# An order table of 1036 steps for the attention, gating and first expert units of a fused attention and two-layer-expert kernel

## The chip, the cores and the metric

The kernel runs on one core of one Trainium2 chip. Its time is the device time of one execution in microseconds (us). The core has five engines with instruction queues of their own: TensorE (PE, with its weight loads shown apart as PEld), VectorE (DVE), ScalarE (ACT), GpSimd (POOL) and SyncE (SP, which here only issues transfers). Each queue is worked off in the order in which the program wrote it; the engines wait for each other through semaphores.

## The reference

Three stages follow each other. The first is a linear attention with random features over 4 batches, 8 heads, 576 tokens and head size 64; its result is laid out as 2304 tokens of 512 numbers. The second is a mixture of eight experts in which each token takes the one expert with the largest logit. The third is a plain two-layer network with a squared ReLU.

```python
def phi(x):
    proj = np.einsum('bhsd,md->bhsm', x, omega)
    h = proj - np.sum(x * x, axis=-1, keepdims=True) / 2.0
    return np.exp(h - np.max(h, axis=-1, keepdims=True)) / np.sqrt(m)
kv, z = np.einsum('bhsm,bhsd->bhmd', k_p, v), np.sum(k_p, axis=2)
num, den = np.einsum('bhsm,bhmd->bhsd', q_p, kv), np.einsum('bhsm,bhm->bhs', q_p, z)
x = num / (den + 1e-06)
...
expert_idx = np.argmax(x @ w_gate, axis=1)
out[mask] = gate_w[mask, None] * (np.maximum(xe @ w1[e], 0.0) @ w2[e])
...
h = np.maximum(x @ w_in, 0.0)
return h * h @ w_out
```

## The kernel before

The 2304 tokens are cut into 18 tiles of 128; a batch is four and a half tiles, so tiles 4 and 13 belong to two batches. Every tile passes through the attention twice, as keys (`kp`) and as queries (`qp`).

Of a key tile: TensorE projects it into two banks of the accumulator memory (`proj`, L250), VectorE takes the maximum of each head (`most`, L265, twice), and adds it to half the squared length of the row (`shift` L271, `shifted` L278; the squares come from GpSimd, L197 and L199, and are summed by VectorE at L211, or, for the first five tiles, come from TensorE at L229). ScalarE takes the exponentials of eight heads (`expo`, L291, 8 instructions), and TensorE adds the tile's share to its batch's key-value sums (`kv_part`, L306). When a batch is complete, `kv_close` copies the sums out (L320, L321) and `kvg_turn` and `kvg` (L329, L331, L338, L345) work the gate's weights into them.

A query tile is projected in the same way; then TensorE transposes the exponentials, in two halves (`t_step`, L354), they are copied out (L356), multiplied with the key-value sums (`n_step`, L372), divided on VectorE (`n_den`, `n_rec`, `n_out`, `n_lg`: L386, L390, L396, L401), transposed again (`x_step`, L412) and copied by ScalarE into `xT` (L416), where the experts read them.

The gating makes of the logits the expert of each token, counts per batch the tokens of each expert on TensorE (L502 takes the count), and loads the weights of the batch's busiest expert. An expert unit is a first product (`layer1`, L874 to L876), a split of its result in a high part on ScalarE (L886) and a low part on VectorE (L887), and a second product (`layer2`, L902 to L904). There are 64 such units, numbered from 0; after the second product of each, `extras` issues the loads and splits planned for that unit.

The order of all this is written out in loops in `attention`: five key tiles ahead, then 13 rounds, each with one query tile s, the key tile s + 5 and the later steps of query tiles s - 1 and s - 2, then rounds of query tiles alone, into which the first units and the gating are written by hand. Eight banks are used under fixed names: `k0`, `k1` for key projections, `q0`, `q1` for query projections, `w0`, `w1` for the key-value sums, `t0`, `t1` for transposes and products. So `x_step` and the first half of `n_step` take the same bank:

```python
ps = self.bank("t0", f"x_ps{t}")      # x_step
ps = self.bank(f"t{i}", f"n_ps{t}_{i}")   # n_step
```

An instruction that writes a bank waits until those that read what was there before are done. The transfers of keys, queries and values are issued on SP's queue in the order of the loops; a load waits for its buffer (four for key columns, three for query columns, two for rows, six for values).

Of the kernel before, what the change touches and what calls it, by code (L numbers as in the profile page):

```python
# [15 lines left out]
P = 128  # L16
# [13 lines left out]
SCALE = float(D) ** -0.25  # L30
HW = 96
# [13 lines left out]
F64_MOST = 122880.0 - 2.0 ** -7  # L45

# [45 lines left out]
class Kern:  # L92
# [92 lines left out]
    def load_rows(self, tag, t):  # L185
        if t >= NT:
            return
        pool = self.kpool if tag == "kp" else self.qpool
        x = pool.tile([P, DM], F32, tag=tag + "r", name=f"{tag}r{t}", bufs=2)
        self.nc.sync.dma_start(out=x, in_=self.a["kk" if tag == "kp" else "qq"][t, :, 1, :])  # L190
        self.rows[tag, t] = x

    def squares(self, tag, t):
        if t >= NT:
            return
        x = self.rows[tag, t]
        self.nc.gpsimd.tensor_tensor(x, x, x, ALU.mult)  # L197
        v = x.rearrange("p (h d) -> p h d", h=H)
# [7 lines left out]
    def sums(self, tag, t):  # L206
        if t >= NT:
            return
        sq = self.rows.pop((tag, t)).rearrange("p (h d) -> p h d", h=H)[:, :, 0:32]
        ssq = self.qpool.tile([P, H, 1], F32, tag="ssq", name=f"ssq_{tag}{t}", bufs=3)  # L210
        self.nc.vector.tensor_reduce(ssq, sq, axis=AX.X, op=ALU.add)  # L211
        three = self.trio(tag, t)
        self.nc.gpsimd.tensor_scalar(three[:, :, 1:2], ssq, -0.5 * SCALE * SCALE, None, op0=ALU.mult)
        self.load_rows(tag, t + 2)
        self.squares(tag, t + 1)

    def colsquares(self, t):
        x = self.cols["kp", t]
# [12 lines left out]
    def colsum(self, tag, t):  # L231
        if t > 4:
            return
        at = 4 * VW + SUMS_AT[t]
        ps = self.kv_ps[0, t % 2][:, at : at + H]
        three = self.trio("kp", t)
        self.nc.vector.tensor_copy(three[:, :, 1:2], ps.rearrange("p (h o) -> p h o", o=1))

    def proj(self, tag, t, banks):

        nc = self.nc
        if t >= NT:
            return
        x = self.cols.pop((tag, t))
# [34 lines left out]

    def expo(self, tag, t, r):  # L280

        nc = self.nc
        if t >= NT:
            return
        ps, bias = self.pj[tag, t], self.bias[tag, t]
        if r == 0:
            pool, to = (self.kpool, self.kp) if tag == "kp" else (self.qpool, self.qp)
            to[t] = pool.tile([P, H, M], F32, tag=tag, name=f"{tag}{t}", bufs=3 if tag == "kp" else 2)
        y = (self.kp if tag == "kp" else self.qp)[t]
        for h in range(r, H, 2):  # L290
            nc.scalar.activation(y[:, h, :], ps[r][:, h // 2 * M : (h // 2 + 1) * M], AF.Exp, bias=bias[:, h : h + 1])  # L291
# [4 lines left out]
    def kv_part(self, b, t, i):  # L296
# [18 lines left out]
    def kv_close(self, b):  # L315
        kv = self.kv[b] = self.qpool.tile([P, 2, 4, XW], F32, tag="kv", name=f"kv{b}", bufs=2)
        self.kvn = self.qpool.tile([P, 2, 4, D], F32, tag="kvn", name=f"kvn{b}", bufs=1)
        for i in range(2):
            ps = self.kv_ps[b, i][:, : 4 * VW].rearrange("p (h w) -> p h w", w=VW)
            self.nc.vector.tensor_copy(kv[:, i, :, 0:VW], ps)  # L320
            (self.nc.vector.tensor_copy if b == 0 else self.nc.scalar.copy)(self.kvn[:, i], ps[:, :, 0:D])  # L321

    def kvg_turn(self, b):

        nc = self.nc
        kvn = self.kvn.rearrange("p a h d -> p (a h d)")
# [76 lines left out]
    def x_step(self, t):
        nc = self.nc
        if not 0 <= t < NT:
            return
        ps = self.bank("t0", f"x_ps{t}")
        for i in range(2):
            x = self.xr.pop((t, i)).rearrange("p h d -> p (h d)")
            for c in range(2):  # L410
                at = (2 * i + c) * P
                nc.tensor.transpose(ps[:, at : at + P], x[:, c * P : (c + 1) * P], self.ident)  # L412
        src = ps.rearrange("p (c t) -> p c t", c=KC)
        for b, lo, hi in pieces(t):
            at = t * P + lo - b * S
            nc.scalar.copy(self.xT[:, b, :, at : at + hi - lo], src[:, :, lo:hi])  # L416
# [997 lines left out]
```

## Time and profile before

| | |
|---|---|
| three timed runs | 739.23, 735.82 and 739.62 us, median 739.23 |
| profiled execution | 734.28 us, of which 732.7 us are the span from its first to its last instruction |
| TensorE busy | 706.8 us (96% of the span), weight loads 683.2 us (93%) |
| VectorE busy | 543.1 us (74%) |
| ScalarE busy | 402.5 us (55%) |
| GpSimd busy | 208.5 us (28%) |
| moved | 132.62 MB, mean 181 GB/s |

Matmuls are pipelined, and the ends of their records are modelled: the start of one group of matmuls to the start of the next tells what a step costs, the busy time does not. The attention with the gating and the first four units takes the first 165.1 us of the span; the remaining 568 us are the other units and the third stage.

### The profile page before, as it was taken

How to read it: one execution, taken by the hardware profiler on the slowest of the kernel's cores; microseconds unless marked ns; L12 is line 12 of the kernel's file. 1: busy time of each engine (PE TensorE's matmuls, PEld its weight loads, DVE VectorE, ACT ScalarE, POOL GpSimd, SP SyncE). 2: the span in 40 equal slices, each digit the busy share in tenths (PEclk: the TensorE clock that was granted, in tenths of full speed). 3: DMA queues.
4: the chain of work that ended last, by engine and by line, in shares of the span. 5: the costliest groups of instructions: out<-in, count | busy, mean ns of one | idle time of the engine just before them, and what ended most of it. 6: DMA issues, size and time to landing. Idle time of an engine off the chain costs nothing. (4 is left out here: it accounts for less than half of the span.)

```text
span 732.7 us, 18313 instructions
## 1 busy us (share of the span) xinstructions
PE 706.8 (96%) x7168; PEld 683.2 (93%) x7168; DVE 543.1 (74%) x1251; ACT 402.5 (55%) x985; POOL 208.5 (28%) x299
## 2 busy tenths in 40 slices
PE   9899998799999999999999999999999999999997
PEld 8778777699999998999999999999999989999997
DVE  4688887687766768855665769687865898888883
ACT  4578778735435534634654645555743455554551
POOL 5556667701100104344730124144331100000000
PEclk9999999999999999999999999999999999999999
DMA  7856654149876686622052556466777374444430
GB/s 232 255 170 197 191 204 142 59 155 332 298 288 223 217 281 209 209 74 66 30 183 99 189 191 217 176 211 218 262 252 228 121 247 140 131 137 135 141 99 32
DMA packets 65372, 132.62 MB, mean 181 GB/s; under 512 B 6113, under 2 KB 25969, under 8 KB 65281
## 3 DMA queue, kind: packets, MB, share of 16 engines
q1 hardware_dynamic: 53024, 88.45, 36.3%
q0 software_dynamic: 12256, 42.95, 17.9%
q8 instruction: 58, 0.95, 0.5%
q14 instruction: 34, 0.27, 0.1%
HBM read 91.05 MB, written 40.32 MB: 179 GB/s over the span
## 5 line engine op out<-in xcount | busy, mean ns | idle before, releaser
L886 ACT ACTIVATE hh<-h 128x288 fp32r<-128x288 f32 x64 | 26.3, 410 | 81.0 <-PE h L876 80.0
L1048 ACT COPY xT<-X 128x288 f32<-128x288 f32 x96 | 37.1, 400 | 39.9 <-PE X L1074 39.4
L1142 ACT CAST hc<-xT 128x384 fp32r<-128x384 f32 (+1 forms) x76 | 39.2, 564 | 29.8 <-DVE xT L65 18.8
L734 POOL DMA_DIRECT2D we<-we x32 | 17.7, 555 | 112.5 <-DVE hl L887 66.6
L291 ACT ACTIVATE kp<-pj_kp,bias_kp 128x128 f32<-128x128 f32 x144 | 39.0, 396 | 13.6 <-DVE bias_kp L278 5.4
L887 DVE SCALAR_TENSOR_TENSOR hl<-h,hh 128x288 fp32r<-128x288 f32 x64 | 29.0, 453 | 21.8 <-ACT hh L886 21.3
L291 ACT ACTIVATE qp<-pj_qp,bias_qp 128x128 f32<-128x128 f32 x144 | 40.7, 389 | 6.8 <-DVE bias_qp L278 6.2
L1188 PE MATMUL y<-wB,hc 128*128 128x256 f32 x152 | 43.2, 284 | 0.0
L1186 PE MATMUL y<-wB,hc 128*128 128x256 f32 x152 | 43.0, 283 | 0.0
L1187 PE MATMUL y<-wB,hc 128*128 128x256 f32 x152 | 43.0, 283 | 0.0
L1144 DVE TENSOR_TENSOR hc<-xT,hc 128x384 fp32r<-128x384 f32 (+1 forms) x76 | 42.2, 617 | 0.0
L838 DVE TENSOR_SCALAR narrow<-narrow 128x512 f32<-128x512 f32 x32 | 15.7, 490 | 34.8 <-ACT narrow L837 34.7
L875 PE MATMUL h<-xl,wA 128*128 128x288 f32 x128 | 38.2, 298 | 1.3 <-DVE xl L863 1.2
L903 PE MATMUL y<-hl,wA 128*128 128x288 f32 x128 | 38.0, 297 | 1.3 <-DVE hl L887 1.3
L1072 PE MATMUL X<-wA,w 128*128 128x288 f32 x128 | 38.0, 297 | 0.5 <-ACT xT L911 0.5
L903 PE MATMUL y<-hl,wB 128*128 128x288 f32 x128 | 38.0, 297 | 0.5 <-DVE hl L887 0.2
L874 PE MATMUL h<-xh,wA 128*128 128x288 f32 x128 | 38.2, 299 | 0.0
L875 PE MATMUL h<-xl,wB 128*128 128x288 f32 x128 | 37.9, 296 | 0.3 <-DVE xl L863 0.3
L902 PE MATMUL y<-hh,wA 128*128 128x288 f32 x128 | 37.9, 296 | 0.0
L1072 PE MATMUL X<-wB,w 128*128 128x288 f32 x128 | 37.9, 296 | 0.0
L874 PE MATMUL h<-xh,wB 128*128 128x288 f32 x128 | 37.8, 296 | 0.0
L1073 PE MATMUL X<-wB,w 128*128 128x288 f32 x128 | 37.8, 295 | 0.0
(255 smaller groups left out, 2819.4 us busy)
## 6 DMA issues: line engine op xcount, KB each, us to landing
hscr<-xT SPq DMA_DIRECT2D x32, 576.0 KB, 3.7
we<-we POOLq DMA_DIRECT2D x32, 512.0 KB, 5.7
xT<-hscr SPq DMA_DIRECT2D x64, 256.0 KB, 4.2
xT<-wscr POOLq DMA_DIRECT2D x48, 256.0 KB, 4.3
wd<-wf SPq DMA_DIRECT2D x22, 512.0 KB, 5.5
wscr<-narrow SPq DMA_DIRECT2D x22, 256.0 KB, 3.6
wd<-wf POOLq DMA_DIRECT2D x10, 512.0 KB, 4.7
kpc<-kk SPq DMA_DIRECT2D x18, 256.0 KB, 3.8
```

Source lines behind the costliest of these rows:

```text
L291: nc.scalar.activation(y[:, h, :], ps[r][:, h // 2 * M : (h // 2 + 1) * M], AF.Exp, bias=bias[:, h : h + 1])
L874: nc.tensor.matmul(ps, w1, xh, start=(c == 0), stop=False)
L875: nc.tensor.matmul(ps, w1, xl, start=False, stop=False)
L902: nc.tensor.matmul(out, w1, hh, start=(f == 0), stop=False)
L903: nc.tensor.matmul(out, w1, hl, start=False, stop=False)
L1072: nc.tensor.matmul(ps, w1, xh[:, r, c], start=(start and c == 0), stop=False, skip_group_check=True)
L1073: nc.tensor.matmul(ps, w1, xl[:, r, c], start=False, stop=False, skip_group_check=True)
L1142: nc.scalar.copy(hc[q].at(0, a, b), raw[:, q, a + 1 : b + 1])
L1144: nc.vector.tensor_tensor(hc[q].at(1, a, b), raw[:, q, a + 1 : b + 1], hc[q].at(0, a, b).bitcast(F32), ALU.subtract)
L1186: nc.tensor.matmul(ps, h1, w1, start=first, stop=False, skip_group_check=True)
L1187: nc.tensor.matmul(ps, h1, w2, start=False, stop=False, skip_group_check=True)
L1188: nc.tensor.matmul(ps, h2, w1, start=False, stop=last, skip_group_check=True)
```

## The change

The loops of `attention` are replaced by a table, `ORDER`, of 1036 words. Each word is a step with its arguments; `attention` walks through the table and calls the method of that name. The steps are the former methods, cut finer: the eight exponentials of a tile are four steps of two, a matmul step and the copy that empties its bank are two steps, the squares and their fold, the sum and its scaling, and the two halves of an expert weight's split are steps of their own. The last argument of a matmul step names the bank, that of a copy the engine (`v` VectorE, `a` ScalarE, `g` GpSimd).

```diff
+ORDER = """
+warm cols:kp:0 proj:kp:0:k colsquare:0 colsums:0 most:kp:0:0 most:kp:0:1 take:0 cols:kp:1 colsquare:1 shift:kp:0
...
+out:14:0 proj:qp:16:w most:qp:16:0 exp:qp:15:0 logit:14:0 exp:qp:15:1 expert_load:0:3 xturn:13:0:k1 exp:qp:15:2
...
+    def copy(self, name, out, x):
+        e = self.engine(name)
+        (e.copy if name == "a" else e.tensor_copy)(out, x)
...
-    def t_step(self, t, i, tag, copy):
...
-        ps = self.bank(f"{tag}{i}", f"t_ps{t}_{i}")
...
-        self.tps[t, i] = lambda: copy(out, ps)
...
+    def turn(self, t, i, bank):
+
         qp = self.qp[t]
+        ps = self.tps[t, i] = self.bank(bank, f"t_ps{t}_{i}")
...
+    def turned(self, t, i, e):
         out = self.qpT[t, i] = self.qpool.tile([P, 512], F32, tag=f"qpT{i}", name=f"qpT{t}_{i}", bufs=2)
+        self.copy(e, out, self.tps.pop((t, i)))
...
-        ps = self.bank(f"t{i}", f"n_ps{t}_{i}")
+        ps = self.bank(bank, f"n_ps{t}_{i}")
...
+    def xturn(self, t, i, bank):
+        if t not in self.xps:
+            self.xps[t] = self.bank(bank, f"x_ps{t}")
...
+    def xtake(self, t, j, e):
+        b, lo, hi = pieces(t)[j]
+        at = t * P + lo - b * S
+        self.copy(e, self.xT[:, b, :, at : at + hi - lo], self.xps[t].rearrange("p (c t) -> p c t", c=KC)[:, :, lo:hi])
...
-    def attention(self, beside):
...
+    def attention(self, more):
+
+        for step in ORDER.split():
+            name, *args = step.split(":")
+            (more.get(name) or getattr(self, name))(*(int(x) if x.isdigit() else x for x in args))
```

The table ends with the `extras` of unit 3; from unit 5's first product on, both programs hold the same steps in the same order. TensorE has 5395 instructions and SP 185 in both. What differs is where copies run: of the 36 copies of transposed queries 7 run on VectorE (20 before) and 29 on ScalarE (16 before); of the 20 copies into `xT` 5 go to VectorE; of the 8 copies of key-value sums 5 go to ScalarE; of the 8 copies without the sums of keys 6 are on VectorE (2 before); one of the four copies of turned sums goes to VectorE and one of the four of gate sums to ScalarE. In the counting of three batches one instruction takes the place of two, as it was for the first batch, and two subtractions of the gating go to GpSimd.

On TensorE, before, these rows stand one after the other for query tiles 13 and 14 (`t_ps` is the transpose of a tile's exponentials, `x_ps` that of its result, `n_ps` the product with the key-value sums):

```order
L354 MATMUL t_ps14_1_2790<-ident_58,qp14_2714 128x128 x4
L354 MATMUL t_ps14_0_2796<-ident_58,qp14_2714 128x128 x4
L412 MATMUL x_ps13_2804<-ident_58,xr13_0_2746 128x128 x2
L412 MATMUL x_ps13_2804<-ident_58,xr13_1_2750 128x128 x2
L372 MATMUL n_ps14_0_2820<-kv3_2587,qpT14_0_2801 64x73 x8
L372 MATMUL n_ps14_1_2829<-kv3_2587,qpT14_1_2795 64x73 x8
```

Now, at the same place in the program, after the projection of query tile 16:

```order
L500 MATMUL x_ps13_2854<-ident_58,xr13_0_2797 128x128 x2
L457 MATMUL t_ps15_0_2859<-ident_58,qp15_2846 128x128 x4
L457 MATMUL t_ps15_1_2872<-ident_58,qp15_2846 128x128 x4
L500 MATMUL x_ps13_2854<-ident_58,xr13_1_2803 128x128 x2
L500 MATMUL x_ps14_2881<-ident_58,xr14_0_2825 128x128 x2
L500 MATMUL x_ps14_2881<-ident_58,xr14_1_2805 128x128 x2
```

The products of tile 15 come only after the projection of tile 17 that follows these rows, and the table gives them banks `t1` and `k1`, while tile 14's result is turned in `t0`.

On ScalarE, before, one round of the 13 (query tile 8 with key tile 13; `qpT` is the copy of transposed exponentials, `xT` that of a result) reads:

```order
L416 COPY xT_113<-x_ps6_1732 128x4x128
L291 ACTIVATE qp8_1787<-pj_qp8_0_1712,bias_qp8_1750 128x128 x4
L356 COPY qpT7_0_1803<-t_ps7_0_1798 128x512
L291 ACTIVATE qp8_1787<-pj_qp8_1_1713,bias_qp8_1750 128x128 x4
L291 ACTIVATE kp13_1866<-pj_kp13_0_1759,bias_kp13_1855 128x128 x4
L291 ACTIVATE kp13_1866<-pj_kp13_1_1760,bias_kp13_1855 128x128 x4
L416 COPY xT_113<-x_ps7_1897 128x4x128
```

Now the same stretch of ScalarE's queue reads:

```order
L281 COPY qpT7_1_1733<-t_ps7_1_1728 128x512
L391 ACTIVATE qp8_1741<-pj_qp8_0_1667,bias_qp8_1739 128x128 x2
L391 ACTIVATE qp8_1741<-pj_qp8_1_1668,bias_qp8_1739 128x128 x4
L281 COPY qpT7_0_1789<-t_ps7_0_1784 128x512
L281 COPY qpT8_0_1798<-t_ps8_0_1793 128x512
L391 ACTIVATE qp8_1741<-pj_qp8_0_1667,bias_qp8_1739 128x128 x2
L391 ACTIVATE kp13_1821<-pj_kp13_1_1745,bias_kp13_1817 128x128 x2
L391 ACTIVATE kp13_1821<-pj_kp13_0_1744,bias_kp13_1817 128x128 x4
L391 ACTIVATE kp13_1821<-pj_kp13_1_1745,bias_kp13_1817 128x128 x2
L281 COPY qpT8_1_1889<-t_ps8_1_1884 128x512
L281 COPY xT_113<-x_ps7_1894 128x4x128
```

Both halves of a transposed tile are now copied by ScalarE here, two of the copies stand between exponentials of one tile, and tile 6's copy into `xT` has gone to VectorE.

## Rows read from the trace of the kernel before

**Rows 1.** Stretches: length; PE, PEld, DVE, ACT, POOL busy; clock, DMA share, GB/s
```profile
0.00:43.01 43.01, 37.98 (x761) 33.31 (x761) 26.40 (x91) 23.79 (x83) 22.81 (x37) 0.96 0.72 224
43.01:113.69 70.68, 66.96 (x1469) 56.15 (x1466) 60.00 (x210) 57.21 (x189) 43.77 (x67) 1.00 0.61 194
113.69:135.83 22.14, 17.95 (x353) 15.40 (x349) 16.49 (x60) 18.56 (x55) 17.45 (x21) 1.00 0.40 127
135.83:165.10 29.27, 26.18 (x289) 24.63 (x287) 21.89 (x78) 14.63 (x32) 7.57 (x8) 1.00 0.32 112
165.10:732.70 567.60, 557.74 (x4310) 553.68 (x4308) 418.34 (x813) 288.28 (x627) 116.95 (x169) 1.00 0.55 182
```

**Rows 2.** Timeline of TensorE: start, length, step, matmul records; one undisturbed round
```profile
37.13 1.10 PE L250 MATMUL pj_qp<-wom,qpc 64*64 64x128 f32 x32
38.17 0.66 PE L412 MATMUL x_ps<-ident,xr 128*128 128x128 f32 x4
38.75 1.10 PE L250 MATMUL pj_kp<-wom,kpc 64*64 64x128 f32 x32
39.79 1.09 PE L354 MATMUL t_ps<-ident,qp 128*128 128x128 f32 x8
40.81 1.15 PE L306 MATMUL kv_ps<-vin,kp 128*64 128x65 f32 x32
41.83 1.25 PE L372 MATMUL n_ps<-kv,qpT 128*64 128x73 f32 x32
```

**Rows 3.** Timeline of TensorE, the early part, with idle time before a step
```profile
21.88 2.09 PE L306 MATMUL kv_ps<-vin,kp 128*64 128x65 f32 x64 [1.41 <-DMA kpc<-kk]
...
27.75 0.41 PE L329 MATMUL kvT_ps<-ident,kvn 128*128 128x128 f32 x2 [0.79 <-DVE kvn L321]
...
28.70 2.55 PE L250 MATMUL pj_kp<-wom,kpc 64*64 64x128 f32 x32
31.17 1.79 PE L354 MATMUL t_ps<-ident,qp 128*128 128x128 f32 x8
```

**Rows 4.** Windows as in rows 1, five and ten us long
```profile
30.00:35.00 5.00, 4.68 (x66) 4.26 (x60) 3.04 (x8) 2.18 (x8) 4.00 (x6) 0.73 0.62 201
170.00:180.00 10.00, 9.42 (x71) 9.19 (x70) 7.84 (x13) 7.74 (x16) 0.78 (x2) 1.00 1.04 390
```

**Rows 5.** Waits of TensorE's weight loads, 43.01 to 113.69: us in total, times, longest
```profile
PEld pj_kp L250 <- ACT kp L291: 3.1, 7, 0.5
PEld n_ps L372 <- ACT qpT L356: 1.5, 2, 1.1
```

**Rows 6.** Waits of TensorE, 113.69 to 165.1: us in total, times, longest
```profile
PE n_ps L372 <- ACT xT L416: 4.7, 6, 1.1
PE cnt_ps L501 <- DVE cnt L502: 0.9, 1, 0.9
```

**Rows 7.** Waits of ScalarE, 43 to 113
```profile
ACT qp L291 <- DVE bias_qp L278: 4.2, 6, 1.2
ACT kp L291 <- DVE bias_kp L278: 4.1, 6, 1.2
```

**Rows 8.** Groups by line, 0 to 165: busy us, mean ns, idle before
```profile
L356 DVE COPY qpT<-t_ps 128x512 f32<-128x512 f32 x20 | 13.7, 687 | 5.8 <-PE t_ps L354 5.6
L356 ACT COPY qpT<-t_ps 128x512 f32<-128x512 f32 x16 | 9.6, 597 | 2.1 <-PE t_ps L354 1.8
L416 ACT COPY xT<-x_ps 128x512 f32<-128x512 f32 (+1 forms) x20 | 11.2, 569 | 5.2 <-PE x_ps L412 5.2
```

**Rows 9.** Timeline: TensorE's first projection and ScalarE's first exponentials
```profile
5.44 1.10 PE L250 MATMUL pj_kp<-wom,kpc 64*64 64x128 f32 x32
...
9.75 6.31 ACT L291 ACTIVATE kp<-pj_kp,bias_kp 128x128 f32<-128x128 f32 x24
```

**Rows 10.** Timeline of TensorE around the end of the fourth unit
```profile
163.52 0.30 PE L902 MATMUL y<-hh,wA 128*128 128x288 f32 x1
...
165.10 0.29 PE L874 MATMUL h<-xh,wA 128*128 128x288 f32 x1
```

More of the change, by code (lines that the diff above doesn't have):

```diff
@@ L30 @@
 SCALE = float(D) ** -0.25
+GROUPS = ((0, 5), (5, 14), (14, NT))
 HW = 96
@@ new lines @@
+exp:qp:1:2 turn:1:0:w1 num:0:1:w0 exp:qp:1:3 cols:qp:2 most:kp:6:0 most:kp:6:1 den:0:0 rec:0:0 shift:kp:6 bias:kp:6
+exp:qp:1:1 turned:1:0:a exp:kp:6:0 den:0:1 turn:1:1:t1 turned:1:1:a rows:qp:3 square:qp:3 fold:qp:3 out:0:0 exp:kp:6:1
+rec:0:1 sum:qp:3 logit:0:0 exp:kp:6:3 out:0:1 vals:5 proj:qp:2:q most:qp:2:0 most:qp:2:1 shift:qp:2 rows:kp:7
+square:kp:7 fold:kp:7 cols:kp:7 sum:kp:7 bias:qp:2 num:1:0:t0 den:1:0 exp:kp:6:2 num:1:1:t1 xturn:0:0:w1 xturn:0:1:w1
+den:1:1 logit:0:1 rec:1:0 logit:1:0 proj:kp:7:k xtake:0:0:a kvs:1:4:1 kvs:1:5:1 exp:qp:2:1 scale:kp:7 most:kp:7:0
@@ new lines @@
+most:kp:7:1 shift:kp:7 rec:1:1 bias:kp:7 rows:qp:4 square:qp:4 exp:qp:2:0 out:1:0 exp:qp:2:2 kvs:1:4:0 cols:qp:3
+kvs:1:5:0 exp:qp:2:3 exp:kp:7:3 rows:qp:5 proj:qp:3:q scale:qp:3 logit:1:1 exp:kp:7:2 out:1:1 turn:2:0:t0 exp:kp:7:0
+square:qp:5 exp:kp:7:1 fold:qp:4 cols:kp:8 most:qp:3:0 xturn:1:0:k1 xturn:1:1:k1 xtake:1:0:a turn:2:1:t1 turned:2:1:a
+rows:kp:8 sum:qp:4 most:qp:3:1 shift:qp:3 proj:kp:8:k bias:qp:3 exp:qp:3:0 turned:2:0:a exp:qp:3:3 vals:6 square:kp:8
+fold:kp:8 sum:kp:8 rows:kp:9 vals:7 num:2:1:t1 cols:qp:4 rows:kp:10 exp:qp:3:1 kvs:1:6:1 cols:kp:9 scale:kp:8
@@ new lines @@
+shift:kp:9 kvs:1:7:1 kvs:1:8:1 kv_nums:1:1:v kvs:1:8:0 kv_take:1:0:a bias:kp:9 exp:kp:9:0 exp:kp:9:1 rec:3:0 out:3:0
+kv_nums:1:0:v scale:qp:5 exp:kp:9:2 rows:qp:6 num:3:1:t1 cols:qp:5 proj:qp:5:q den:3:1 logit:3:0 rec:3:1 square:qp:6
+fold:qp:6 sum:qp:6 rows:kp:12 square:kp:12 fold:kp:12 most:qp:5:0 most:qp:5:1 scale:qp:6 shift:qp:5 exp:kp:9:3
+cols:kp:10 rows:kp:11 square:kp:11 rows:qp:7 square:qp:7 kv_turn:1:w0 kv_turned:1:a turn:4:1:t0 turned:4:1:a
+fold:kp:11 out:3:1 kv_take:1:1:a bias:qp:5 exp:qp:5:2 exp:qp:5:0 exp:qp:5:1 proj:kp:10:k most:kp:10:0 cols:qp:6
@@ new lines @@
+logit:3:1 most:kp:10:1 sum:kp:12 shift:kp:10 bias:kp:10 exp:qp:5:3 vals:10 kvg:1:w0 kvg_take:1:v xturn:3:0:t0
+xturn:3:1:t0 turn:4:0:t1 turned:4:0:v turn:5:0:w1 exp:kp:10:1 fold:qp:7 sum:kp:11 scale:kp:11 turned:5:0:a sum:qp:7
+cols:kp:11 exp:kp:10:0 proj:qp:6:q most:qp:6:0 num:4:0:w0 den:4:0 rows:qp:8 vals:9 most:qp:6:1 exp:kp:10:2 num:4:1:w1
+den:4:1 rec:4:1 turn:5:1:t1 square:qp:8 exp:kp:10:3 shift:qp:6 bias:qp:6 xtake:3:0:a turned:5:1:a logit:4:1 out:4:1
+proj:kp:11:k exp:qp:6:0 exp:qp:6:2 rec:4:0 rows:kp:13 most:kp:11:0 square:kp:13 fold:kp:13 exp:qp:6:1 cols:qp:7
@@ new lines @@
+num:5:1:t0 exp:qp:6:3 den:5:1 most:kp:11:1 scale:kp:12 cols:kp:12 rec:5:1 turn:6:0:w1 shift:kp:11 bias:kp:11 logit:4:0
+scale:qp:7 num:5:0:t1 den:5:0 rec:5:0 proj:qp:7:q exp:kp:11:2 exp:kp:11:0 exp:kp:11:1 out:4:0 exp:kp:11:3 logit:5:0
+out:5:1 xturn:4:0:w0 xturn:4:1:w0 xtake:4:1:a fold:qp:8 xtake:4:0:a out:5:0 logits:0:g turn:6:1:t1 most:qp:7:0
+rows:qp:9 square:qp:9 turned:6:0:a logit:5:1 most:qp:7:1 turned:6:1:a shift:qp:7 proj:kp:12:k xturn:5:0:w0 cols:qp:8
+cols:qp:9 sum:qp:8 bias:qp:7 exp:qp:7:3 xturn:5:1:w0 most:kp:12:0 xtake:5:0:a vals:13 top_logit:0 most:kp:12:1
@@ new lines @@
+exp:qp:7:1 sum:kp:13 rows:kp:14 num:6:0:t0 exp:qp:7:0 den:6:0 fold:qp:9 num:6:1:t1 sum:qp:9 den:6:1 kvs:2:9:1
+exp:qp:7:2 cols:kp:13 kvs:2:9:0 vals:11 shift:kp:12 rec:6:1 kvs:2:10:0 kvs:2:10:1 below_top:0:g ranks:0 scale:qp:8
+proj:qp:8:q logit:6:1 bias:kp:12 top_rank:0 exp:kp:12:3 square:kp:14 exp:kp:12:2 fold:kp:14 scale:kp:13 choice:0
+rec:6:0 count:0:k1 rows:qp:11 exp:kp:12:0 square:qp:11 rows:qp:10 out:6:1 exp:kp:12:1 out:6:0 logit:6:0 xturn:6:0:t0
+vals:12 xturn:6:1:t0 turn:7:1:t1 turned:7:1:a most:qp:8:0 count_take:0 most:qp:8:1 shift:qp:8 bias:qp:8 exp:qp:8:0
@@ new lines @@
+proj:kp:13:k xtake:6:0:v most:kp:13:0 most_tokens:0 exp:qp:8:2 exp:qp:8:3 most:kp:13:1 count_ranks:0 fold:qp:11
+cols:kp:14 kvs:2:11:1 turn:7:0:t1 turned:7:0:a sum:kp:14 turn:8:0:t0 turned:8:0:a num:7:1:q1 exp:qp:8:1 count_top:0
+shift:kp:13 den:7:1 rec:7:1 bias:kp:13 rows:kp:15 exp:kp:13:3 exp:kp:13:1 exp:kp:13:0 logit:7:1 out:7:1 num:7:0:t1
+kvs:2:11:0 cols:kp:15 den:7:0 rec:7:0 out:7:0 scale:kp:14 proj:qp:9:q scale:qp:9 exp:kp:13:2 cols:kp:16 logit:7:0
+sum:qp:11 turn:8:1:t0 turned:8:1:a most:qp:9:0 square:qp:10 fold:qp:10 xturn:7:0:t1 sum:qp:10 most:qp:9:1 shift:qp:9
@@ new lines @@
+expert_high:0:0 fold:qp:13 logit:9:1 sum:qp:13 proj:qp:11:q most:qp:11:0 scale:kp:16 turn:10:0:t1 den:10:1
+most:qp:11:1 xtake:8:0:a vals:15 shift:qp:11 vals:17 turned:10:0:a rows:qp:15 bias:qp:11 exp:qp:11:2 square:kp:17
+xturn:9:0:t0 xturn:9:1:t0 rec:10:1 out:10:1 fold:kp:17 logit:10:1 exp:qp:11:0 exp:qp:11:1 proj:kp:16:k most:kp:16:0
+most:kp:16:1 square:qp:14 fold:qp:14 kvs:3:13:1 exp:qp:11:3 num:10:0:t1 den:10:0 xtake:9:0:a shift:kp:16 rec:10:0
+bias:kp:16 kvs:3:13:0 exp:kp:16:0 kvs:3:14:0 kvs:3:14:1 exp:kp:16:1 logit:10:0 out:10:0 scale:qp:12 exp:kp:16:2
@@ new lines @@
+exp:kp:17:0 bias:qp:13 fold:qp:15 sum:qp:15 cols:qp:14 kvs:3:16:0 exp:kp:17:2 kvs:3:17:0 kv_take:3:0:v turned:11:0:a
+num:11:0:t0 den:11:0 scale:qp:14 rec:11:0 logit:11:0 out:11:0 k_done rows:qp:17 turned:12:0:a num:12:0:t1 den:12:0
+kv_take:3:1:a turn:12:1:w1 square:qp:16 turned:12:1:v kv_nums:3:0:a rec:12:0 kv_turn:3:w0 kv_turned:3:v exp:qp:13:1
+exp:qp:13:0 out:12:0 logit:12:0 exp:qp:13:3 xhigh:0:0:1 xhigh:0:0:0 xturn:11:0:q0 xturn:11:1:q0 exp:qp:13:2
+proj:qp:14:k most:qp:14:0 expert_high:0:1 num:12:1:w0 most:qp:14:1 shift:qp:14 bias:qp:14 den:12:1 rec:12:1
@@ L403, in x_step, with logit @@
[L403 to L416, printed above, removed]
+    def logit(self, t, i):
+        self.nc.vector.tensor_tensor(self.lgh[:, t, i], self.nps[t, i][:, :, VW:], self.rd[t, i].to_broadcast([P, 4, E]), ALU.mult)
```

628 lines of the change are left out of this document (226 added, 402 removed).

## Prediction

> **What bounds the kernel now.** I read the windows first, cut at four starts of a query projection (tiles 3, 13, 17) and at the first product of unit 5, where the table ends [rows 1]. Behind 165.10 us TensorE is busy for 557.74 of 567.60 us, and both programs hold the same order there: whatever the change gives, it gives ahead of 165.10, as an earlier start of unit 5.
>
> Ahead of it no engine is full. In the longest stretch, 43.01 to 113.69, VectorE works 60.00 and ScalarE 57.21 of 70.68 us [rows 1]. TensorE shows 66.96, but its ends are modelled, so I take its work from starts instead. The timeline has a round without a wait [rows 2]: projection 1.04 us (38.75 to 39.79), turning four heads twice 1.02 (0.51 each), one tile's share of the key-value sums 1.02 (0.51 a half), turning the result 0.58 (0.29 a half), the products 1.18 (41.83 to 43.01, the next mark of rows 1; 0.59 a half). The round lasts 5.88 us, and ten such are 58.8. Two batches are closed in the stretch; turning four blocks and multiplying with the gate I estimate by x_ps and t_ps at 0.6 and 1.0, so 3.2 for two. That makes 62.0 of work and 8.7 of stalls in 70.68.
>
> By the Trainium skill (Perfetto Trace Analysis, Identifying the Most-Contended Engine) matmul busy time is no measure of headroom, the busy share of weight loads is. By matmul busy ahead of 165.10 (149.07 us, from rows 1) at most 16.0 could be won; by weight loads (129.47) 35.6. The trace agrees that they disagree: the starts give a figure in between (24.3, below).
>
> Next the waits: who holds up TensorE. In the rounds it is the bank of the key projection, not yet read by ScalarE's exponentials (7 times, 3.1 us), and the copied transposes (1.5) [rows 5]. From 113.69 on it is the products, which share bank `t0` with the turned result that ScalarE has still to copy into `xT` (6 times, 4.7), and the counting (0.9) [rows 6]. Early, TensorE stood 1.41 us before a key-value share, 0.79 at the first batch's turn, and the projection at 28.70 took 2.47 us, to 31.17 [rows 3], where rows 2 have 1.04; the granted clock of 30 to 35 is 0.73 [rows 4], so part of this stretch ran at the lower of the two levels, 1.2 GHz, after the idling before it.
>
> **The change, stretch by stretch.** Same matmuls, so TensorE's floor for each stretch is a count of the table's steps times the costs above.
>
> *To the projection of query tile 3 (43.01 now).* The table puts 11 projections, 5 sums of squares (8 matmul records each, taken like 8 of t_ps at 1.02), 14 halves of key-value shares, 4 turns, 4 products, 2 turned results and one batch's turn and gate ahead: 11.4 + 5.1 + 7.1 + 2.0 + 2.4 + 0.6 + 1.6 = 30.2 us from the first projection at 5.44 [rows 9], so 35.6. ScalarE starts at 9.75 and needs 0.263 for one exponential (6.31 for 24) [rows 9]; 82 of them are 21.6, seven copies at 0.57 to 0.6 [rows 8] at most 4.2, so 35.5. Two engines end together; the closing of the first batch goes from TensorE to VectorE, back, to ScalarE and back, and cannot be hidden wholly. I leave 2.4 us for it: 38.0, that is 5.0 less. The slow projection at 28.70 is inside this: it cost 2.47 - 1.04 = 1.4, and if the clock falls again, that comes back.
>
> *Tile 3 to tile 13 (70.68).* 20 projections, 20 turns, 20 halves of results, 19 products, 23 halves of shares, two closings: 20.8 + 10.2 + 5.8 + 11.2 + 11.7 + 3.2 + one count (0.3) = 63.2. ScalarE gets 6 copies of transposes more (6 x 0.597 [rows 8] = 3.6), two of key-value sums and a gate copy (no row on ScalarE: between nothing and 0.6 each, the copy of 512 columns; I take 0.5), one less into `xT` (0.57) and three fewer small ones (at most 0.57 each, I take 0.4): 57.21 + 3.6 + 1.5 - 0.6 - 1.2 = 60.5. VectorE loses 7 copies of 0.687 [rows 8] and gets one into `xT` of the same size, and one small one more: about 56. So TensorE becomes the fullest at 63.2. Its stalls of 8.7 do not vanish, since three engines at 56 to 63 must fit together: I leave not quite half, 3.9, by the size of what is named in rows 5 (4.6), which the order moves, against the rest, which rows 5 do not name and which I leave. 67.1, 3.6 less.
>
> *Tile 13 to tile 17 (22.14).* TensorE: 4.2 + 4.1 + 1.5 + 4.1 + 2.3 + 1.6 = 17.8. ScalarE: 18.56, and 4 copies of transposes more, two or three of `xT` fewer: about 18.7. The wait for `xT` (0.78 each, four of the six) goes: the turned result of tile 14 is in `t0`, the next products are in other banks and a projection later. 20.5, so 1.6 less.
>
> *Tile 17 to unit 5 (29.27).* One projection, 6 products, 4 turns, 6 halves of results, three counts (0.3 each), nine halves of units at 1.58 [rows 10]: 1.0 + 3.5 + 2.0 + 1.7 + 0.9 + 14.2 = 23.3. Two `xT` waits, the count's 0.9 and the chain of the last tile stand in the other 6.0. The table puts two first products between them and the counts apart; the last tile's chain is as long as before. I leave 2.3: 25.6, 3.7 less.
>
> Floors: 35.6 + 63.2 + 18.7 + 23.3 = 140.8, that is 24.3 below 165.10. Taken: 38.0 + 67.1 + 20.5 + 25.6 = 151.2, 13.9 below.
>
> What costs nothing: the finer cut adds no instruction to the exponentials (two per step, eight per tile). Transfers are as many as before; their queue could stall only where a load waits for a buffer, and by the table every buffer comes free 4 us or more of TensorE's work ahead of the load's use. If that cover went, each would cost its landing time; rows 3 have one such wait, 1.41. Two units' `extras` come closer to each other; where a narrowing's load lands late, ScalarE's next split stands behind it, but TensorE has three halves of units (4.7 us) before it needs that.
>
> The profiled execution took 734.28, 4.95 below the median of the three timed runs; their mean is 738.2. The sum is 734.28 - 13.9 = 720.4 in the profile's frame and 738.2 - 13.9 = 724.3 in that of the timed runs. I predict 724.
>
> **The rivals.**
>
> *The banks still bind.* The same gap comes back round after round at the key projection [rows 5], there are eight banks before and after, and both projections keep their pairs. Then stretches two and three stay, and only the first and last give: 8.7, so 729.5. Against it: in the late stretch banks stand free. The skill's rule (Perfetto Trace Analysis, Optimization Strategy) is that a gap which repeats can mean that there isn't room for the next tile; no order cures that. By that rule this rival is the outcome; the trace bears it out for 3.1 of the 8.7 us.
>
> *ScalarE keeps its idle time.* In stretches two and three it idles 13.47 and 3.58. If these come from chains that the order does not shorten, its added work lengthens them: 74.0 and 22.3, 3.5 more than now; with 8.7 from the others 5.2 remain: 733.
>
> *Slower: exponentials wait for their bias.* ScalarE waited 12 times for VectorE's bias in 20 tiles, 8.3 us in all [rows 7], 0.42 a tile. Now copies which TensorE needs stand between a tile's exponentials in a fixed queue; a late bias stops them too. The other idle time kept, the gain is 13.5 - 20w for a wait w per tile: none at 0.68, slower by half a per cent from 0.86. At the longest wait seen, 1.2, it loses 10.5: 749. For it: every engine is fuller. Against: VectorE, which makes the bias, loses work.
>
> *Given back later.* From 170 to 180 the transfers' share is 1.04 and TensorE falls to 9.42 of 10 [rows 4]. Were the units bound by weights there, an earlier start would win nothing: 738. Against: the loads are planned by unit, so they start earlier too, and TensorE idles 9.86 in all of the 567.60 us.
>
> **How the numbers follow.** The sum as taken 0.52 (its own range 718 to 731: half of the stalls that I left gone too, or half of the gain), banks 0.20, ScalarE idle 0.12, slower 0.08, given back 0.08. Half a per cent, 3.7 us, is about what can be told from no change. The first three are faster, less 0.04 for their upper edges: 0.80; same 0.12; slower 0.08. The range runs from near the floors (738.2 - 22 = 716) to just under no change, 737; it leaves out the slower case and the given-back one.
>
> **What would show it.** Right: unit 5's first product starts at about 151 instead of 165.10; query projections 3, 13, 17 at about 38, 105 and 126; the wait of the products for `xT` gone from TensorE's list; no half-speed stretch before 40; ScalarE above 0.88 busy from tile 3 to 13. Wrong: rounds still near 7 us with key projections waiting for exponentials (banks); ScalarE's waits for the bias above 0.7 a tile; or unit 5 early and the end not.

## The result and the profile after

The changed kernel takes 715.07 us (median of four runs, 714.05 to 720.08) against 739.19 of the kernel before: 24 us less. By the means (716.07 against 738.46) the ratio is 0.970, 95% interval 0.964 to 0.975, so 3.0% faster. I forecast 724, range 716 to 737: the direction was right, the gain was larger, and the median lies 0.9 us under the range, the mean just inside it. Profile against profile, the execution of 714.05 us stands 20.2 below the former 734.28; the sum had said 13.9.

The page's first lines (busy time, share of the span, instructions): TensorE's busy time has fallen by 8.3 us from 706.8, with as many matmuls; its share of the span has risen from 96 to 98%.

```profile
span 712.4 us, 18287 instructions
PE 698.5 (98%) x7168; PEld 679.8 (95%) x7168; DVE 540.1 (76%) x1237; ACT 404.4 (57%) x994; POOL 208.7 (29%) x301
```

The windows of the same five stretches as [rows 1], cut at the starts of query projections 3, 13 and 17 and at the product that stood at 165.10:

```profile
0.00:36.88 36.88, 34.37 (x728) 30.53 (x728) 25.59 (x96) 26.15 (x91) 23.46 (x37) 1.00 0.72 232
36.88:99.49 62.61, 62.52 (x1468) 55.09 (x1466) 55.59 (x194) 58.10 (x193) 44.88 (x71) 1.00 0.73 229
99.49:116.75 17.26, 17.26 (x353) 15.39 (x349) 15.34 (x57) 16.35 (x49) 10.45 (x12) 1.00 0.38 121
116.75:144.46 27.71, 27.26 (x320) 25.62 (x320) 24.14 (x82) 15.74 (x38) 13.14 (x15) 1.00 0.48 162
144.46:712.40 567.94, 557.05 (x4310) 553.23 (x4308) 419.47 (x812) 288.07 (x627) 116.80 (x168) 1.00 0.55 182
```

The stretches are 6.13, 8.07, 4.88 and 1.56 us shorter, 20.64 in all; the rest, 567.94 against 567.60, gives 0.34 back. Over all the traces of this document the rest, which holds the same steps in every kernel, takes from 566.2 to 573.6 us, so 0.34 can't be told from nothing, and the start of this product compares two orders more closely than the whole time does. In the second and third stretch TensorE's busy time fills the window, and the clock column is 1.00 everywhere, where the first stretch had 0.96.

TensorE's waits from 36.88 to 144.46 (us in total, times, longest) have one row of a named engine left; the 4.7 for `xT` [rows 6] are gone, and of the key projections' waits for ScalarE's exponentials [rows 5] 0.2 of 3.1 is left. ScalarE's waits for the bias, 8.3 us in [rows 7], have one row too (36.88 to 99.49):

```profile
PE x_ps L500 <- DVE xr L489: 0.4, 1, 0.4
```

```profile
ACT qp L391 <- DVE bias_qp L380: 0.4, 1, 0.4
```

A round of the changed kernel on TensorE's timeline, from the step behind query projection 3 (36.88) to query projection 4:

```profile
37.92 0.66 PE L457 MATMUL t_ps<-ident,qp 128*128 128x128 f32 x4
38.41 0.60 PE L500 MATMUL x_ps<-ident,xr 128*128 128x128 f32 x4
38.85 0.60 PE L457 MATMUL t_ps<-ident,qp 128*128 128x128 f32 x4
39.38 1.41 PE L358 MATMUL pj_kp<-wom,kpc 64*64 64x128 f32 x32
40.72 0.73 PE L470 MATMUL n_ps<-kv,qpT 128*64 128x73 f32 x16
41.28 0.64 PE L406 MATMUL kv_ps<-vin,kp 128*64 128x65 f32 x16
41.74 0.69 PE L470 MATMUL n_ps<-kv,qpT 128*64 128x73 f32 x16
42.26 1.10 PE L406 MATMUL kv_ps<-vin,kp 128*64 128x65 f32 x32
43.30 1.10 PE L358 MATMUL pj_qp<-wom,qpc 64*64 64x128 f32 x32
```

No row has idle time ahead of it (the key projection takes 0.3 us longer to its next step than in [rows 2]); the halves of the transposes and products stand apart, with another step of TensorE between them while the other engines empty the bank.

### The profile page after: what moved, and what is told of

The parts are those of the page before. It is cut to its first block, busy times and chain, and to the rows that moved or that the text cites. A ratio compares the mean times of both kernels' runs of the same rounds, so it can differ in the third digit from the quotient of the medians.

```text
span 712.4 us, 18287 instructions
## 1 busy us (share of the span) xinstructions
PE 698.5 (98%) x7168; PEld 679.8 (95%) x7168; DVE 540.1 (76%) x1237; ACT 404.4 (57%) x994; POOL 208.7 (29%) x301
## 4 chain that ended last, share of the span: by engine, by line
PE 88%; DMA 4%; DVE 3%; ACT 3%; issue 1%; SPq 0%; ACTq 0%; POOLq 0%; POOL 0%; DVEq 0%
PE y L1108 7%; PE y L1106 7%; PE y L1107 7%; PE X L992 5%; PE X L994 5%; PE X L993 5%; PE y L827 3%; PE h L782 3%; PE h L783 3%; PE h L781 3%; PE y L828 3%; PE y L826 3%; PE kv_ps L406 3%; PE pj_kp L358 3%; PE n_ps L470 3%; PE pj_qp L358 2%
## 5 line engine op out<-in xcount | busy, mean ns | idle before, releaser
L798 DVE SCALAR_TENSOR_TENSOR hl<-h,hh 128x288 fp32r<-128x288 f32 x64 | 29.0, 453 | 20.5 <-ACT hh L792 19.6
L971 DVE SCALAR_TENSOR_TENSOR xT<-xT 128x288 f32<-128x288 f32 (+1 forms) x64 | 38.3, 636 | 0.0
L781 PE MATMUL h<-xh,wA 128*128 128x288 f32 x128 | 38.0, 297 | 0.0
L992 PE MATMUL X<-wB,w 128*128 128x288 f32 x128 | 37.9, 296 | 0.0
L783 PE MATMUL h<-xh,wA 128*128 128x288 f32 x128 | 37.8, 295 | 0.0
```

The source lines that it names most:

```text
L781: nc.tensor.matmul(ps, w1, xh, start=(c == 0), stop=False)
L783: nc.tensor.matmul(ps, w2, xh, start=False, stop=(c == KC - 1))
L971: nc.vector.scalar_tensor_tensor(v, v, 0.0, v, op0=ALU.max, op1=ALU.mult)
L992: nc.tensor.matmul(ps, w1, xh[:, r, c], start=(start and c == 0), stop=False, skip_group_check=True)
```

## The experiments

A cheap reading would be that the order did it, since it is most of the diff. So the first runs keep the order and take away one of the other parts, or the reverse. "Unit 6" is the start of the mark's product (165.10 before, 144.46 after); "tile 3" and the two columns behind it are the lengths of the first three stretches. Stretches and marks are in us and come from one profiled execution each. Times are medians, ratios are to the kernel before on the same chip.

| kernel | us | ratio, 95% | tile 3 | 3 to 13 | 13 to 17 | unit 6 |
|---|---|---|---|---|---|---|
| before | 739.19 | | 43.01 | 70.68 | 22.14 | 165.10 |
| changed | 715.07 | 0.970 (0.964 to 0.975) | 36.88 | 62.61 | 17.26 | 144.46 |
| changed, former engines | 735.02 | 0.996 (0.994 to 0.998) | 39.43 | 70.68 | 24.34 | 164.99 |
| changed, former engines for `qpT` only | 726.12 | 0.983 (0.978 to 0.988) | 39.07 | 69.14 | 19.37 | 156.20 |
| changed, former banks | 765.69 | 1.039 (1.034 to 1.044) | 46.32 | 89.76 | 26.42 | 193.53 |
| changed, exponentials whole | 721.67 | 0.980 (0.975 to 0.984) | 38.14 | 65.86 | 17.40 | 149.10 |
| changed, TensorE's halves joined | 736.46 | 0.999 (0.997 to 1.001) | 40.78 | 74.20 | 20.75 | 164.34 |
| before, new engines | 740.40 | 1.002 (0.999 to 1.004) | 44.07 | 73.72 | 23.34 | 170.07 |
| before, `x_ps` 12 to 14 elsewhere | 737.67 | 0.998 (0.996 to 1.001) | 42.81 | 70.71 | 22.14 | 164.94 |

**Former engines in the new order.** 35 words of the table get another last letter, of this kind:

```diff
-turned:5:1:a
+turned:5:1:v
-xtake:6:0:v
+xtake:6:0:a
```

> The changed order, banks and all, but 35 copies run on the engine that had them before (transposed queries half on VectorE, all copies into xT on ScalarE). Theory A, the order alone took the stalls away: VectorE is then busy for about 60 of the 62.6 us from query tile 3 to tile 13 and ScalarE for about 54, TensorE stays the fullest, and the first product of unit 6 starts at 144.5 to 146 us; time 714 to 717. Theory B, moving copies from VectorE to ScalarE was needed: the stretch goes half of the way back to 70.7, unit 6 starts at 149 or later, time 719 or more.

Measured 735.02, unit 6 at 164.99: in the profile the whole gain up to the mark is gone, and by the timed runs 0.4% of the 3.0% is left. The order alone (theory A) is not enough.

**The new engines in the former order.** In the kernel before, each of these copies asks a list for its engine:

```diff
-        self.tps[t, i] = lambda: copy(out, ps)
+        self.tps[t, i] = lambda: eng_copy(self.nc, f"turned:{t}:{i}", out, ps)
```

> The kernel before with its own order and banks; only the engines of the copies are those of the changed kernel. Theory A, order: no gain, time 736 to 742, the first product of unit 6 at 164 to 168 us, since ScalarE's queue is fuller and TensorE waits for it as before. Theory B, engines: half of the 20.6 us come from this, time 726 to 732.

740.40, no gain: theory B falls as well, if it means engines alone. (The mark's 170.07 is from the slowest of ten runs, 743.60; the ratio of 1.002 shows no loss.) ScalarE's wait for the bias stays at 8.1 us although VectorE works less, 55.79 us instead of 60.00 (44 to 118):

```profile
ACT kp L298 <- DVE bias_kp L285: 4.5, 8, 1.2
ACT qp L298 <- DVE bias_qp L285: 3.6, 5, 0.8
```

**Only the copies of transposed queries back.** As in the first experiment, but for `turned` alone (19 words: 16 to VectorE, 3 to ScalarE).

> The changed kernel with only the copies of transposed queries on their former engines (16 from ScalarE to VectorE, 3 back; 13 more on VectorE, 9 us). All 35 copies together cost 20 us. If VectorE's load is the cause: most of that, unit 6's first product at 158 or later, 728 or more. If it was the closing of the batches and the copies into xT: at most 5 us, unit 6 before 150, 720 or less.

Unit 6 at 156.20, 11.7 us of the 20.5 that all the engines cost: between the two marks expected (158 or later, before 150), nearer to the first. The second stretch, and ScalarE's waits in it:

```profile
39.07:108.21 69.14, 64.83 (x1468) 56.01 (x1466) 59.35 (x202) 54.37 (x187) 44.94 (x71) 1.00 0.67 211
```

```profile
ACT qp L391 <- DVE bias_qp L380: 6.5, 6, 2.0
ACT qp L391 <- PE pj_kp L358: 3.1, 1, 3.1
ACT kp L391 <- DVE bias_kp L380: 2.5, 2, 1.7
```

VectorE works 59.35 us, nearly what it did before (60.00), and the bias is late again, 9.0 us in all. One place shows how, by VectorE's queue and then TensorE's:

```profile
74.44 0.69 DVE L281 COPY qpT<-t_ps 128x512 f32<-128x512 f32 x1 [1.33 <-PE t_ps L457]
75.05 0.68 DVE L370 TENSOR_REDUCE three_qp<-pj_qp 128x4 f32<-128x512 f32 x1
75.64 0.14 DVE L579 COPY cnt<-cnt_ps 1x8 f32<-1x8 f32 x1
```

```profile
74.33 0.43 PE L358 MATMUL pj_kp<-wom,kpc 64*64 64x128 f32 x2
75.84 1.10 PE L358 MATMUL pj_kp<-wom,kpc 64*64 64x128 f32 x30 [1.08 <-DVE cnt L579]
```

The copy put on VectorE waited 1.33 us for its transpose. Behind it stood the maxima, which the bias needs, and the 0.14 us copy of the count, which holds bank `k1`; the key projection needs that bank and stood 1.08 us. That points to the place of a step in VectorE's queue more than to the load: in the former order, with 55.79 us of load, the bias was late by 8.1 us too.

**Former banks in the new order.** 76 bank names differ. Where a bank is not yet read in the program's order, the step goes later; 317 of the 1036 steps change place, 92 of them to a later one, by up to 25 places:

```diff
-xturn:1:0:k1 xturn:1:1:k1 xtake:1:0:a turn:2:1:t1 turned:2:1:a ... turned:2:0:a exp:qp:3:3
+turn:2:1:t1 turned:2:1:a ... turned:2:0:a xturn:1:0:t0 xturn:1:1:t0 xtake:1:0:a exp:qp:3:3
```

> The changed order and engines, but every matmul step takes the bank with the fixed name that it had before; 76 bank names differ, and where the bank is not yet read in the program's order, a step goes up to 25 places later. Theory A, order alone: unit 6 starts within 2 us of 144.5, time 714 to 717. Theory C, the free choice of banks is half of it: the products wait again for the copy into xT (4.7 us before in the late part) and the key projections' neighbours for copies, unit 6 starts at 149 or later, time 719 or more.

765.69, slower than both kernels. Theory C is right in kind, and the loss is far above its mark of 149; what part of it the moved steps have isn't known. The granted clock was low here for part of the time (the column before the last two):

```profile
0.00:46.32 46.32, 38.14 (x729) 33.08 (x729) 25.70 (x96) 25.00 (x86) 25.17 (x39) 0.89 0.58 193
46.32:136.08 89.76, 72.04 (x1470) 60.08 (x1466) 56.46 (x193) 60.09 (x197) 42.98 (x68) 0.90 0.50 157
```

**Another bank in the former order.** The counterpart, on the wait that my forecast priced:

```diff
-        ps = self.bank("t0", f"x_ps{t}")
+        ps = self.bank("w1" if t == 13 else "w0" if t in (12, 14) else "t0", f"x_ps{t}")
```

> The kernel before, but the turned results of query tiles 12 to 14 go to banks w0 and w1, which stand empty there, in place of t0, which the next products need. Three of the six waits for the copy into xT (4.7 us in all, 0.78 each) can vanish. Theory C, banks: unit 6 starts 2.3 us earlier, at 162.8, time 2 us lower. Theory A, order: the wait only moves to what comes next on TensorE (the next projection's bank or the copy of the transposed queries), and unit 6 starts less than 1 us earlier.

TensorE's waits from 113 to 165.0:

```profile
PE n_ps L372 <- ACT xT L416: 2.5, 3, 1.1
PE t_ps L354 <- ACT qp L291: 1.6, 3, 0.8
PE n_ps L372 <- DVE qpT L356: 1.2, 1, 1.2
```

Three of the six waits for `xT` went, 2.2 us; the products' wait for `qpT` is 0.8 longer than before and the transposes' for the exponentials too, and the stretch from tile 13 to 17 is 22.14 in both. The wait moved to the next thing that was late, as theory A expected.

**Exponentials whole.** The four pairs of a tile stand together, for instance:

```diff
-exp:qp:3:0 turned:2:0:a exp:qp:3:3 ... exp:qp:3:1 ... exp:qp:3:2
+exp:qp:3:0 exp:qp:3:3 exp:qp:3:1 exp:qp:3:2 turned:2:0:a
```

> The changed order, but the four pairs of exponentials of a tile stand together, where the first pair stood or as soon after it as the banks allow. Theory A in its plain form, only the distance between a step and what needs it matters: at most 1.5 us later, time 714 to 716.5. Theory D, the fine cut matters, since a copy that TensorE needs can otherwise stand behind 2.1 us of exponentials: the waits of products and transposes for copies come back at 0.3 to 0.5 a tile, unit 6 starts 4 us or more later, time 718 or more.

Unit 6 4.6 us later, 721.67: theory D. ScalarE in this kernel, and the product on TensorE that waits for the copy:

```profile
41.42 2.17 ACT L392 ACTIVATE qp<-pj_qp,bias_qp 128x128 f32<-128x128 f32 x8
43.43 0.64 ACT L282 COPY qpT<-t_ps 128x512 f32<-128x512 f32 x1
```

```profile
44.12 0.73 PE L471 MATMUL n_ps<-kv,qpT 128*64 128x73 f32 x16 [0.95 <-ACT qpT L282]
```

The same place of the changed kernel, where the copy goes between two and six exponentials and TensorE has no wait:

```profile
40.17 0.63 ACT L391 ACTIVATE qp<-pj_qp,bias_qp 128x128 f32<-128x128 f32 x2
40.68 0.59 ACT L281 COPY qpT<-t_ps 128x512 f32<-128x512 f32 x1
41.15 1.68 ACT L391 ACTIVATE qp<-pj_qp,bias_qp 128x128 f32<-128x128 f32 x6
```

**TensorE's halves joined.** 22 of 54 pairs of halves stood apart, now one; steps that depend on them follow, and 550 steps in all change place:

```diff
-turn:6:0:w1 ... proj:qp:7:q ... turn:6:1:t1 ... turned:6:0:a
+proj:qp:7:q ... turn:6:0:w1 turn:6:1:t1 ... turned:6:0:a
```

> The changed order, but on TensorE the two halves of every transpose, product and turned result stand together as before (22 of 54 pairs stood apart; now one). Theory A: at most 1 us later, time 714 to 716.5. Theory D, the fine cut matters on TensorE too: the second half waits for its copy about 0.3 us each, 5 us or more later, time 719 or more.

736.46, the gain is gone, some 20 us where 5 or more were expected. TensorE's timeline at one of the dearest places, a copy of ScalarE there, and TensorE's windows over it:

```profile
59.85 1.09 PE L458 MATMUL t_ps<-ident,qp 128*128 128x128 f32 x8
62.18 0.66 PE L458 MATMUL t_ps<-ident,qp 128*128 128x128 f32 x4 [1.24 <-ACT xT L282]
64.00 1.11 PE L458 MATMUL t_ps<-ident,qp 128*128 128x128 f32 x4 [1.16 <-ACT qpT L282]
65.90 2.22 PE L471 MATMUL n_ps<-kv,qpT 128*64 128x73 f32 x32 [0.78 <-DVE qpT L282]
68.05 1.99 PE L359 MATMUL pj_kp<-wom,kpc 64*64 64x128 f32 x32
```

```profile
62.87 1.07 ACT L282 COPY qpT<-t_ps 128x512 f32<-128x512 f32 x2 [0.74 <-PE t_ps L458]
```

```profile
60.00:62.00 2.00, 0.94 (x8) 0.70 (x7) 1.59 (x4) 1.77 (x6) 0.97 (x2) 1.00 0.88 197
62.00:64.00 2.00, 0.66 (x4) 0.42 (x5) 0.00 (x0) 1.25 (x4) 1.69 (x5) 1.00 0.90 291
64.00:66.00 2.00, 1.22 (x6) 0.82 (x8) 0.69 (x1) 2.00 (x8) 0.62 (x1) 0.51 1.05 348
66.00:68.00 2.00, 2.00 (x32) 1.90 (x32) 0.16 (x1) 0.02 (x1) 0.00 (x0) 0.50 1.04 283
68.00:70.00 2.00, 2.00 (x36) 1.63 (x34) 0.95 (x5) 0.00 (x0) 0.00 (x0) 0.50 0.30 106
70.00:72.00 2.00, 2.00 (x52) 1.92 (x52) 1.71 (x6) 0.00 (x0) 0.00 (x0) 0.78 0.00 0
```

Four halves of transposes stand in a row; two of them need a bank that a copy of ScalarE has not yet emptied, and the product behind them a copy of VectorE. TensorE waits on ScalarE (1.24 us), ScalarE on TensorE (0.74), TensorE on ScalarE again (1.16), and from 64 on the granted clock is at the level of 1.2 GHz.

**Who is full now.** Four kernels take work away from the changed one, and one adds some. The edits: half of a key share's matmuls for its first half; a ScalarE copy more per tile; exponentials over 64 columns (into fixed buffers); maxima over 64 columns; and the three shortenings together, there with both halves of the key share.

```diff
-        for j in range(4):
+        for j in range(2 if t not in (tiles[0], tiles[-1]) and i == 0 else 4):
...
+        if i == 0 and 3 <= t <= 12:
+            self.nc.scalar.copy(self.spare, out[:, 0:256])
...
+            n = M // 2 if (3 <= t <= 12 if tag == "qp" else t >= 8) else M
...
+        n = M // 2 if r == 0 and (3 <= t <= 12 if tag == "qp" else t >= 8) else M
```

> The changed kernel with part of TensorE's work left out: in the first half of a key tile's share of the key-value sums (heads 0 to 3), 4 of the 8 matmuls are left out for the tiles inside a batch, so the output is another. About 0.25 us less for each of some 9 steps from query tile 3 to 13. If TensorE is what bounds that stretch: 62.6 becomes 60.3 to 60.7. If ScalarE (58.1 busy) or the chains between engines bound it: 62.0 or more.

> The changed kernel with one more ScalarE copy of 256 columns behind the copy of the transposed queries of tiles 3 to 12 (0.3 to 0.4 us each, 3 to 4 us more on ScalarE between query tiles 3 and 13, 61 to 62 of 62.6). If TensorE alone bounds the stretch and ScalarE's idle time is free: at most 0.5 us longer. If ScalarE's idle time is bound to chains: longer by the added 3 to 4 us, 65.5 to 66.5.

> The changed kernel with less work on ScalarE: the exponentials of query tiles 3 to 12 and key tiles 8 to 17 cover 64 of 128 columns (the rest keeps old values, so the output is another), some 160 instructions in the stretch from query tile 3 to 13, at 0.05 us less each by the copies of 256 and 512 columns (0.41 and 0.60): about 7.6 us less, 50.5 of 62.6. If ScalarE is what the others wait for: the stretch falls to 60.5 or less. If TensorE's own work is the limit (theory A as forecast): 62 to 63. If the order fits these durations and no others: longer than 62.6.

> The changed kernel with less work on VectorE: the first maximum of query tiles 3 to 12 and key tiles 8 to 17 looks at 64 of 128 columns of each head (the output is another), 20 instructions in the stretch at about 0.26 us less: some 5 us less of 55.6. If VectorE's chain, maximum to bias to exponentials, is what the others wait for: the stretch from query tile 3 to 13 falls from 62.6 to 61 or less. If TensorE is full: 62 to 63.

> The changed kernel with less work on all three: both shortenings, and half of the matmuls of a key tile's share of the key-value sums for the tiles inside a batch, both halves (about 0.5 us a tile, 4.5 us of TensorE's in the stretch; the output is another). Theory F, the stretch is as long as its fullest engine: TensorE's own 62.6 minus 4.5, so 58 to 58.6 from query tile 3 to 13. Theory L, chains of steps between the engines set the pace of the rounds, whatever the engines' loads: above 60.5.

They take 715.33, 721.52, 717.08, 715.54 and 710.19 us, by two runs each. The windows from query tile 3 to 13, in this order (62.61 us in the changed kernel):

```profile
35.74:99.21 63.47, 62.10 (x1414) 53.78 (x1410) 56.20 (x197) 58.31 (x194) 45.82 (x72) 1.00 0.70 229
```

```profile
37.39:102.36 64.97, 63.84 (x1468) 55.54 (x1466) 55.70 (x193) 60.33 (x200) 44.82 (x70) 1.00 0.70 222
```

```profile
36.24:98.79 62.55, 62.38 (x1470) 55.02 (x1466) 56.68 (x196) 51.33 (x194) 45.87 (x72) 1.00 0.75 235
```

```profile
36.44:99.10 62.66, 62.58 (x1469) 55.13 (x1467) 51.17 (x195) 58.02 (x195) 45.10 (x71) 1.00 0.73 232
```

```profile
36.44:96.30 59.86, 59.66 (x1351) 51.58 (x1347) 51.37 (x198) 51.24 (x195) 45.42 (x71) 1.00 0.76 243
```

Less of ScalarE (6.8 us) or of VectorE (4.4 us) leaves the stretch as long as it was, so neither of them by itself sets its length. Less of TensorE alone gives nothing either, where 60.3 to 60.7 were expected if TensorE alone set it (63.47; unit 6 at 144.11): its transposes then wait 1.4 us for ScalarE's exponentials and two key shares 1.1 for nothing that the profile names. With all three lighter the stretch falls by 2.75, of 3.7 us of matmuls left out (117 of 1468 records, 32 of which take 1.02 in [rows 2]): under theory L's 60.5, over the 58 to 58.6 of theory F, and 0.9 above what theory F makes of the matmuls that really went, 58.9. One ScalarE copy more per tile, 0.41 us each or 4.1 in all, cost 4.2 us at unit 6 (148.65). So the order stands at the point where TensorE is just full and the steps of the other engines are close behind it, and ScalarE's idle time is no room for work put in at another place.

## Why the prediction was right, and where its size was off

**The term that was off** is the stalls that I left in: 2.4, 3.9, 1.8 and 2.3, that is 10.4 us. By stretch:

| | floor | forecast | measured |
|---|---|---|---|
| to tile 3 | 35.6 | 38.0 | 36.88 |
| 3 to 13 | 63.2 | 67.1 | 62.61 |
| 13 to 17 | 18.7 (TensorE 17.8) | 20.5 | 17.26 |
| 17 to the mark | 23.3 (rightly 26.5) | 25.6 | 27.71 |

Above TensorE's floors, with the last one put right, 1.3, nothing, nothing and 1.2 us were left (the two in the middle end 0.6 and 0.5 under their floors, so the prices from one round are a little high). "I leave not quite half ... against the rest, which rows 5 do not name" kept stalls on the ground that the list of waits did not name them. TensorE was the fullest at my 63.2, as the step said, and the lighter kernels show that neither ScalarE's nor VectorE's load by itself held it up. The part that rows 5 do not name fits ScalarE's late bias [rows 7]: 8.3 us before, 0.4 after, 9.0 once VectorE has its copies back. I had that wait only as the slower rival. It is not the only way to lose the gain: with joined halves ScalarE waits 2.6 us for the bias (40.8 to 115), and the gain is gone as well.

**A wrong label.** The product at 165.10 is unit 6's first, and five units are done there, not four; unit 5's stood at 161.93 before and 141.28 after; the mark itself is the same product in both programs. The last floor so lacked two halves of units, 3.2 us, which hid part of the other error: 151.2 + 3.2 - 9.0 of stalls - 0.9 (the third floor by TensorE instead of ScalarE) is the measured 144.5. With the right label the forecast would have been 727.5; that the slip brought it nearer was luck.

**Two sums.** ScalarE's floor from tile 13 to 17 does not come out of its terms: 18.56, four copies more (2.4) and two or three fewer (1.1 to 1.7) make 19.2 to 19.8, not 18.7. Measured are 16.35 us, with TensorE full at 17.26, so this load was no floor. The weight loads ahead of 165.10 add up to 129.49, not 129.47, which leaves the 35.6 as it is; of the two bounds from busy time, the won 20.6 passed the 16.0 and stayed far under the 35.6.

**ScalarE's and VectorE's loads** from tile 3 to 13 were forecast at 60.5 and 56: 58.10 and 55.59. ScalarE above 0.88 busy: 0.93. No half-speed before 40: right, 1.00.

**A wait taken for its price.** "The wait for `xT` (0.78 each, four of the six) goes" was right, but of the two reasons given, another bank and a later place, the bank buys nothing by itself: in the former order three such waits went and the stretch stayed at 22.14.

**The rivals.** Banks still bind: no, the repeated gap went with the same eight banks. By the Trainium skill (Perfetto Trace Analysis, Optimization Strategy) a repeating gap can mean that there isn't room for the next tile. Here the trace shows that there was room, 3.1 us of waits before and 0.2 after; under the former bank names this order takes 765.7 us. ScalarE keeps its idle time: no, from tile 3 to 13 it idles 4.51 us where it idled 13.47. Slower by the bias: no, 0.02 us a tile. Given back: 0.34 us.

**What the gain came from.** I had costed the order, the banks, the engines and the cut apart. None of them stands alone: the new order with the former engines gives 0.1 us at unit 6, the former order with the new engines gives nothing, and joined halves or former banks take back 19.9 and more than all of it. By the Trainium skill (Perfetto Trace Analysis, Optimizing Scalar/DVE Operations) offloading some work to ScalarE may make sense if VectorE is saturated, and breaking up instructions may let work be completed sooner. For the engines the traces agree only within this order, and VectorE was at 60.00 of 70.68 us, so not quite full. No run here breaks up an exponential; what was worth 4.6 us is a copy put between whole ones.

**Open.** Each of these kernels keeps an order drawn up for other engines, banks or cuts, and three of them (former banks, whole exponentials, joined halves) move further steps, so that their losses are not those of banks, cut or halves alone; whether an order drawn up anew for, say, the former engines would reach the same time wasn't tried. So the 20.6 us can't be shared out among the parts.

## What to carry to other kernels

Where three engines with in-order queues are some 80 to 90% busy, as here before (57.21, 60.00 and about 62.0 of 70.68 us), sum each engine's work per stretch. If a new order is fitted to engine, bank and place together, the stretch can come down to the fullest engine's sum, as it did here, not only half of the way. A wait in the list is not its price: without a change of what comes next, it moves. And such an order is brittle: moving about one copy per tile (19 words) cost more than half of the gain, so after any later change of a step it is worth drawing the order up again.

## What the runs showed of the hardware

In the kernel with joined halves TensorE was busy for 0.94 and 0.66 us of the 2 us from 60 and from 62, and the granted clock then stood at 0.5, the level of 1.2 GHz, for some 7 us, although TensorE was full again from 66 on; the key projection at 68.05 took 1.91 us to the next step where it has 1.04. By the clock column (0.49, 0.50, 0.50 and 0.22 of 2 us each) this cost at most 3.4 us of work, and some 0.4 less where TensorE idled at the low clock (1.22 of 2 us busy from 64): about as much as the three waits there, 3.2 us. With the former banks the clock took at most 14 of the 49 us (0.11 of 46.32 and 0.10 of 89.76), with the former engines at most 3.5 of the 20.5 (0.93 in 24.34 and 0.94 in 30.54 us). So part of what these kernels lost is the clock's price for their stalls, in the changed kernel it is nothing (1.00 throughout), and my sum had 1.4 us for the clock in all.
